# A streamed-weight ring on Trainium2: alternating its fetches between SyncE's hardware queue and GpSimd's software queue

## The chip, the cores and the metric

One core of one Trainium2 chip. The metric is the time of one execution on the device, in microseconds (us); lower is better. Each kernel was executed several times, and each execution has a state (fast or slow, by its time against the fastest of the same kernel). All times below are medians.

## The reference, cut to what matters

Two independent parts write the two halves of the output. Part A (a long convolution) is not touched by the change. Part B is a recurrence over 64 segments of 32 rows, with an 8-row memory carried from one segment to the next:

```python
for s in range(n_seg):                                # 64
    h = concat([mem, x[:, 32*s:32*s+32]], axis=1)     # 40 rows x 1024
    q, k, v = h @ Wq, h @ Wk, h @ Wv                  # 32 heads of 128
    p = softmax(where(mask, q @ k.T * scale, -1e9))
    o = (p @ v) @ Wo
    mem = o[:, :8]                                    # the next segment needs this
    outs.append(o[:, 8:])
```

Every segment needs all four weight matrices, 64 chunks of 128 x 2048 bf16 (512 KB each). They do not all fit on the chip, so some are read again for every segment.

## The kernel before

Of the 64 chunks of a segment, 44 stay in SBUF and 20 are streamed from a DRAM copy `WS` into a ring of four slots. The chunks are used in a fixed order. When TensorE has used a chunk, its slot is free, and the fetch of the chunk four places later is issued:

```python
NSTREAM = 20
RING = 4
...
ring = ctx.enter_context(tc.tile_pool(name="b_ring", bufs=RING))
...
uses = [ch for s in range(n_seg) for ch in order if ch in streamed]

def fetch():
    n = len(loaded)
    if n < len(uses):
        t = ring.tile([128, 2048], BF, tag="wring", name="wring")
        nc.sync.dma_start(t[:], stream_src(uses[n]))        # L576: SyncE, hardware queue
        loaded.append(t)

def done(ch):
    if ch in streamed:
        loaded[used[0]] = None
        used[0] += 1
        fetch()
...
class Proj:                                                 # q, k or v, one half of the heads
    def run(self, n=8):
        for kc in range(self.kc, self.kc + n):
            ch = (self.m, kc, self.g)
            w = weight(ch)
            for c in range(4):
                nc.tensor.matmul(self.acc[32*c:32*c+32, :], lhsT=hT[:, kc, :], rhs=w[:, c*512:(c+1)*512], ...)
            done(ch)
```

Each engine executes its instructions in program order, the issue of a DMA included, so it matters what else stands in GpSimd's order. In a segment, before the change:

```python
for c in range(4):                                          # at the start of the segment
    nc.gpsimd.dma_start(VBs[32*c:32*c+8, :], VBD[s, c])     # L627: values of the memory rows
... # GpSimd also copies a few keys and queries (L631, L638), twice a segment
if s + 1 < n_seg:
    load_x(s + 1)                                           # L600: rec <- REC, on GpSimd
...
nc.gpsimd.dma_start(<32 rows of out>, Y[:])                 # L793: the output of the segment
if j == NB - 1:                                             # in every fourth segment
    ...
    for dq in range(4):                                     # L798: rewrites 8 rows of each of 4 segments
        nc.gpsimd.dma_start(<out rows>, YB[32*dq:32*dq+32, :])
```

`YB` writes rows that `Y` has written, so its first store waits until the `Y` store has landed.

Of the kernel before, what the change touches and what calls it, by code (L numbers as in the profile page):

```python
# [392 lines left out]
def b_kernel(ctx: ExitStack, tc, x, mem0, Wq, Wk, Wv, Wo, outb, n_seg):  # L393
    nc = tc.nc
# [37 lines left out]
    def stream_src(ch):  # L432
        return WS[ring_order.index(ch), :, 0:2048]
# [134 lines left out]
    uses = [ch for s in range(n_seg) for ch in order if ch in streamed]  # L568
# [3 lines left out]
    def fetch():  # L572
        n = len(loaded)
        if n < len(uses):
            t = ring.tile([128, 2048], BF, tag="wring", name="wring")
            nc.sync.dma_start(t[:], stream_src(uses[n]))  # L576
            loaded.append(t)

    def weight(ch):
# [5 lines left out]
# [5 lines that stand above are left out]
# [21 lines left out]
    with tc.manual_schedule():  # L611
        for _ in range(RING):
            fetch()
# [255 lines left out]
```

## Time and profile before

| | before |
|---|---|
| time, median of the first 4 runs | 2673.66 us |
| recurrence, in the profiled run | from about 541 us to 2686 us |
| a segment | 33.3 us (mean spacing of the copies `rec<-y_tp`, one a segment; 32.8 us without the very first, which took 63.6) |
| streamed in a segment | 20 chunks of 512 KB |

First lines of the profile page of the kernel before. In the 40 slices, DMA is the mean busy share of the 16 DMA engines in tenths, and GB/s is what they moved. Then the chain of waits (the work that ended last, followed back), the groups of instructions (`busy, mean ns | idle time just before them <- what ended most of it`), and the DMA issues (`count, KB each, median us from issue to landing`).

```profile
DMA  7886945599999999999999999998999999999996
GB/s 282 307 285 247 345 142 162 176 370 334 332 337 330 348 319 332 338 330 328 329 334 333 329 329 334 329 326 312 330 332 329 328 349 322 346 324 346 334 345 248
...
q1 hardware_dynamic: 265560, 767.19, 80.8%
q0 software_dynamic: 26048, 45.25, 5.0%
...
DMA 56%; PE 31%; issue 3%; DVE 3%; ACT 1%; POOL 1%; SPq 0%; DVEq 0%; ACTq 0%; POOLq 0%
DMA wring<-WS 50%; PE acc L654 14%; PE yacc L740 6%; PE kb_ps L534 4%; PE qk_tp L669 2%; PE vb_ps L547 2%; DMA out_dram<-ot 1%; DMA Wearly<-in_B_Wk_dram 1%; ACT Y L790 1%; DMA pw<-in_B_Wv_dram 1%; PE y_tp L606 1%; DMA X_sb<-in_B_x_dram 1%; 
...
L654 PE MATMUL acc<-wring,rec 128*32 128x512 bf16 x3840 | 419.8, 425 | 371.3 <-DMA wring<-WS 366.3
...
L740 PE MATMUL yacc<-wring,OT 128*32 128x256 bf16 x2560 | 149.7, 293 | 156.4 <-DMA wring<-WS 153.3
...
wring<-WS SPq DMA_DIRECT2D x1280, 512.0 KB, 5.6
```

From slice 9 on, the DMA engines look nearly always busy, at about 330 GB/s. Half of the span lies on the DMA of `wring` in the chain of waits. TensorE, the engine of the matmuls, stood idle 366.3 and 153.3 us until a `wring` DMA had landed. Nearly all bytes are on q1, SyncE's queue; q0 is GpSimd's.

The windows view of the kernel before, over the steady part of the recurrence (columns: stretch, its length, busy us and number of instructions of PE, PEld, DVE, ACT and POOL, granted TensorE clock as a share of full speed, DMA share, GB/s):

```profile
core 0: us, PE busy (x) PEld busy (x) DVE busy (x) ACT busy (x) POOL busy (x), PEclk, DMA share, GB/s
600.00:2500.00 1900.00, 1365.37 (x28828) 682.29 (x28828) 366.19 (x1344) 391.81 (x752) 328.90 (x983) 0.91 0.94 332
```

GpSimd's instructions in order of time, kernel before, around the end of a fourth segment (start, us, instruction; in brackets the idle time before it):

```profile
1493.37 0.76 POOL L793 DMA_DIRECT2D out_dram<-Y  x1 [12.22 <-ACT Y L790]
1497.75 2.35 POOL L798 DMA_DIRECT2D out_dram<-YB  x4 [3.62 <-issue]
1500.09 2.06 POOL L627 DMA_DIRECT2D VBs<-VBD  x4
```

`Y` is issued at 1493.37. The first `YB` store waits 3.62 us; the profile names no releaser in this place. The loads of `VBs` follow only after that. The new segment began at 1493.5, so GpSimd is late by several microseconds, which costs nothing here: no weight fetch stands behind it.

### The profile page before, as it was taken

The page shows a single profiled execution, that of the slowest core. Times are in us where ns is not written, and L with a number is a line of the kernel's source. Part 1 is how long each engine was busy: PE and PEld are TensorE (multiplying, and loading weights), DVE is VectorE, ACT ScalarE, POOL GpSimd, SP SyncE. Part 2 cuts the span into 40 slices and gives each one's busy share as a digit, 9 for nine tenths or more (in the row PEclk, how much of TensorE's full clock was granted, in tenths as well). Part 3 has the DMA queues.
Part 4 walks back from the last instruction along what each step waited for, and adds up shares of the span by engine and source line. Part 5 has one row for each costly group of instructions (what it writes and reads, how often), then busy time and mean ns, then how long its engine had stood idle before and what let it go on. Part 6 is the DMA issues. An engine that isn't in the chain of part 4 may idle for free.

```text
span 2686.0 us, 76248 instructions
## 1 busy us (share of the span) xinstructions
PE 1844.0 (69%) x33598; PEld 904.9 (34%) x33620; DVE 659.9 (25%) x1944; ACT 639.8 (24%) x1143; POOL 461.6 (17%) x1210
## 2 busy tenths in 40 slices
PE   3565298837777767767776777676776767677765
PEld 1221143313333333333333333333433333333333
DVE  5896221101111111111121112111111111111111
ACT  6873011112222222222222222221222222222221
POOL 5043000001211111111111111111111111212111
PEclk9797599968899998989899889888889898998998
DMA  7886945599999999999999999998999999999996
GB/s 282 307 285 247 345 142 162 176 370 334 332 337 330 348 319 332 338 330 328 329 334 333 329 329 334 329 326 312 330 332 329 328 349 322 346 324 346 334 345 248
DMA packets 302324, 841.52 MB, mean 313 GB/s; under 512 B 72396, under 2 KB 84716, under 8 KB 301991
## 3 DMA queue, kind: packets, MB, share of 16 engines
q1 hardware_dynamic: 265560, 767.19, 80.8%
q0 software_dynamic: 26048, 45.25, 5.0%
q10 hardware_dynamic: 10384, 24.20, 2.6%
q8 instruction: 262, 4.29, 0.6%
q14 instruction: 70, 0.57, 0.1%
HBM read 777.14 MB, written 61.87 MB: 312 GB/s over the span
## 4 chain that ended last, share of the span: by engine, by line
DMA 56%; PE 31%; issue 3%; DVE 3%; ACT 1%; POOL 1%; SPq 0%; DVEq 0%; ACTq 0%; POOLq 0%
DMA wring<-WS 50%; PE acc L654 14%; PE yacc L740 6%; PE kb_ps L534 4%; PE qk_tp L669 2%; PE vb_ps L547 2%; DMA out_dram<-ot 1%; DMA Wearly<-in_B_Wk_dram 1%; ACT Y L790 1%; DMA pw<-in_B_Wv_dram 1%; PE y_tp L606 1%; DMA X_sb<-in_B_x_dram 1%; POOL Yre L342 1%; DVE rec L607 0%; DMA Wlate<-in_B_Wv_dram 0%
## 5 line engine op out<-in xcount | busy, mean ns | idle before, releaser
L654 PE MATMUL acc<-wring,rec 128*32 128x512 bf16 x3840 | 419.8, 425 | 371.3 <-DMA wring<-WS 366.3
L654 PEld LDWEIGHTS <-rec 128*32 128x32 bf16 x12288 | 339.9, 103 | 850.0 <-issue 646.3
L663 ACT CAST qkv_sb<-acc 128x512 bf16<-128x512 f32 x384 | 224.7, 585 | 1066.3 <-PE acc L654 1066.3
L654 PE MATMUL acc<-Wearly,rec 128*32 128x512 bf16 x4608 | 436.0, 461 | 32.3 <-DVE rec L607 21.3
L654 PE MATMUL acc<-Wlate,rec 128*32 128x512 bf16 x3840 | 333.3, 390 | 0.0
L740 PEld LDWEIGHTS <-OT 128*32 128x32 bf16 x8192 | 235.5, 100 | 236.2 <-issue 220.1
L740 PE MATMUL yacc<-Wlate,OT 128*32 128x256 bf16 x5632 | 274.0, 286 | 13.0 <-issue 13.0
L740 PE MATMUL yacc<-wring,OT 128*32 128x256 bf16 x2560 | 149.7, 293 | 156.4 <-DMA wring<-WS 153.3
L631 POOL COPY KT<-rec 128x128 bf16<-128x128 bf16 x128 | 38.2, 298 | 710.8 <-PE S L680 635.6
L754 DVE COPY KT<-qk_tp 128x512 bf16<-128x512 bf16 x64 | 27.2, 425 | 514.2 <-PE qk_tp L669 514.2
L793 POOL DMA_DIRECT2D out_dram<-Y x64 | 48.4, 756 | 565.4 <-ACT Y L790 520.9
L627 POOL DMA_DIRECT2D VBs<-VBD x256 | 128.9, 510 | 0.7 <-issue 0.4
L600 POOL DMA_DIRECT2D rec<-REC x64 | 37.2, 581 | 451.4 <-PE acc L654 324.7
L790 ACT CAST Y<-yacc 128x256 bf16<-128x256 f32 x64 | 23.8, 372 | 375.5 <-PE yacc L740 375.5
L607 DVE COPY rec<-y_tp 128x64 bf16<-128x64 bf16 x64 | 12.3, 192 | 410.8 <-PE y_tp L606 402.9
L685 DVE TENSOR_REDUCE mx<-S 128x5 f32<-128x200 f32 x128 | 47.1, 368 | 258.2 <-PE S L680 257.9
L669 PE MATMUL qk_tp<-ident,qkv_sb 128*128 128x128 bf16 x1024 | 108.5, 233 | 0.5 <-ACT KT L763 0.5
L722 ACT CAST OT<-OTp 128x512 bf16<-128x512 f32 x128 | 74.9, 585 | 138.0 <-PE OTp L713 135.8
L740 PE MATMUL yacc<-Wlate,OTB 128*32 128x256 bf16 x1408 | 91.8, 283 | 15.5 <-issue 13.9
L669 PEld LDWEIGHTS <-qkv_sb 128*128 128x128 bf16 x1024 | 62.7, 102 | 109.8 <-issue 82.0
L726 DVE CAST OTB<-OTp 128x128 bf16<-128x128 f32 x128 | 34.7, 271 | 221.9 <-ACT OT L722 221.9
L534 PE MATMUL kb_ps<-XBT,Wearly 128*128 128x512 bf16 x283 | 83.9, 385 | 1.7 <-ACT XBT L501 1.2
(192 smaller groups left out, 2134.6 us busy)
## 6 DMA issues: line engine op xcount, KB each, us to landing
wring<-WS SPq DMA_DIRECT2D x1280, 512.0 KB, 5.6
rec<-REC POOLq DMA_DIRECT2D x64, 192.0 KB, 5.7
SK<-s_sb SPq DMA_DIRECT2D x16, 512.0 KB, 4.1
SU<-s_sb SPq DMA_DIRECT2D x16, 512.0 KB, 3.7
Kg<-SK ACTq DMA_DIRECT2D x32, 256.0 KB, 4.0
Ug<-SU SPq DMA_DIRECT2D x32, 256.0 KB, 5.0
REC<-stage SPq DMA_DIRECT2D x4, 2048.0 KB, 13.2
pw<-in_B_Wv_dram SPq DMA_DIRECT2D x16, 512.0 KB, 6.3
```

What stands on the lines that cost most here:

```text
L534: nc.tensor.matmul(ps[:], lhsT=ws[kc][:, hl * 128:(hl + 1) * 128], rhs=XBT[:, kc].rearrange("p s t -> p (s t)"), start=(kc == 0), stop=(kc ...
L547: nc.tensor.matmul(ps[:], lhsT=XBT[:, kc, 16 * tb:16 * tb + 16, :].rearrange("p s t -> p (s t)"), rhs=ws[kc][:, c * 512:(c + 1) * 512], st ...
L627: nc.gpsimd.dma_start(VBs[32 * c:32 * c + 8, :], VBD[s, c])
L631: nc.gpsimd.tensor_copy(KT[:, :, :, 32:40], KBs[:, 128 * g:128 * g + 128].rearrange("p (c i t) -> p i c t", c=4, i=4))
L654: nc.tensor.matmul(self.acc[32 * c:32 * c + 32, :], lhsT=hT[:, kc, :], rhs=w[:, c * 512:(c + 1) * 512], start=(kc == 0), stop=(kc == 7), t ...
L663: nc.scalar.copy(sb[:], self.acc[:])
L669: nc.tensor.transpose(tp[:, i * 128:(i + 1) * 128], sb[:, i * 128:(i + 1) * 128], ident[:])
L685: nc.vector.tensor_reduce(out=mx[:], in_=S, op=ALU.max, axis=AX.X)
L722: nc.scalar.copy(OT[:], o_view(g)[:, :, :, 0:32])
L740: nc.tensor.matmul(yacc[32 * dq:32 * dq + 32, o:o + 256], lhsT=src, rhs=w[:, hh * 1024 + dq * 256:hh * 1024 + (dq + 1) * 256], start=(h == ...
L790: nc.scalar.copy(Y[:], yacc[:, 0:256])
L793: nc.gpsimd.dma_start(bass.AP(outb.tensor, outb.offset + SEG * s * 2048, [[256, 4], [2048, 32], [1, 256]]), Y[:])
```

## The change

The intent: issue the fetches from two engines, so that two DMA queues work on the stream.

```diff
         n = len(loaded)
         if n < len(uses):
             t = ring.tile([128, 2048], BF, tag="wring", name="wring")
-            nc.sync.dma_start(t[:], stream_src(uses[n]))
+            (nc.sync if n % 2 == 0 else nc.gpsimd).dma_start(t[:], stream_src(uses[n]))
             loaded.append(t)
```

Even chunks stay on SyncE, odd ones go to GpSimd. Bytes, slots and the order of use are the same.

## The prediction

> **What bounds the kernel now.** The recurrence (about 541 to 2675 us of the profiled 2686.0) is paced by streamed weights. The chain of waits puts 50% of the span on the DMA of `wring`. The windows view shows the 16 DMA engines 94% busy there, at 332 GB/s. The memory-row copies (`rec<-y_tp`) come every 33.3 us, one a segment: 20 chunks of 512 KB, 1.65 us each. It is a closed loop of four slots: SyncE issues chunk n+4 about 0.02 us after TensorE's last matmul on chunk n; issue to landing is 5.6 us median (DMA issues view). TensorE waits on `wring` 366+153 us (groups view).
>
> **What changes.** Ten of a segment's 20 chunks move from SyncE's in-order stream to GpSimd's. No byte, buffer or wait is removed. The Trainium skill, "DMA: Bandwidth & Descriptors", section "Issuing engines are not separate DMA queues", says all queues run on the same 16 engines, so I expect no new bandwidth; what is saved is SyncE's 0.32 us of issue a chunk, and SyncE is not the limit. 512 KB issues on GpSimd take 0.53 us in the trace and land about as fast as SyncE's (6.8 and 6.3 us for `pw`; 7.0 and 7.5 for `zt`). GpSimd is 17% busy, so 640 x 0.53 = 340 us more fits; no VectorE lock-out shows: `VBs` issues take 497 to 544 ns throughout.
>
> **What hurts: order on GpSimd.** A fetch now stands behind whatever GpSimd waits for.
> - Three of four segments: after the output `Y`, four `VBs` issues end 2.5 us into the segment; the first odd fetch was issued at 2.8 to 3.0 us. Hardly any delay.
> - After every fourth segment (15 that matter): the four `YB` stores wait until `Y` has landed (about 5 us), then take 2.35 us, then `VBs` 2.1 us. GpSimd is free about 10 us into the next segment, today harmless. Its first odd fetch (index 5), today issued at 2.0 us and used at 8.6 us, is then issued at 10 to 12 us and used at 15 to 17. SyncE can fetch only chunks 4, 6 and 8 meanwhile, since TensorE consumes in order; the DMA engines run dry for 5 to 7 us. Because DMA is the limit, most is not made up: 7 us x 15, about +105 us.
> - The two streams interleave, so an even chunk finishes later than in one first-in-first-out queue; with four slots the loop has little slack. Estimate 0 to +3% of 2130 us; I take +30 us. Two rings may instead hide gaps (the bulk load on two hardware queues at 537 to 566 us reached 387 GB/s), which would offset this.
>
> All of this is on the critical path, because chunk waits are.
>
> **Prediction.** 2673.6 + 105 + 30 = about 2810 us, range 2720 to 2920. Faster by over 2%: 0.05; within 2%: 0.11; slower by over 2%: 0.84.
>
> **What would show it.** Segments following a `YB` store grow from 33.5 to about 40 us, the others by under 1 us; in them the first GpSimd `wring` issue comes 10 to 12 us in, the DMA share dips, and TensorE has one `wring` wait of over 5 us. About 335 MB move from q1 to q0.
>
> **What would make it wrong.** Two rings lifting the rate above 345 GB/s in the other segments (then within 2% or faster); a GpSimd stall that I don't see, such as issues much above 0.53 us or fetches held by earlier software DMAs, adding over 1 us to every segment (then above 2900); or the ring refilling quickly after the gap, so that only 3 us a time is lost.

## The result, and the profile after

| | before | after |
|---|---|---|
| time, median of 4 runs | 2673.66 us | 2862.61 us |
| ratio | | 1.0709 (95% interval 1.0654 to 1.0764) |
| GB/s, 600 to 2500 us | 332 | 306 |
| first memory copy (start of the recurrence) | 541.8 us | 550.9 us |
| segment after a `YB` store (mean of 15) | 31.46 us | 38.30 us |
| the other segments of four, in order | 32.17, 33.09, 34.63 us | 34.21, 33.95, 35.51 us |

A ratio is the mean time of one kernel's fast runs over that of the other's of the same rounds, so it is not quite the ratio of the quoted medians. The segment lengths were worked out from the trace as the spacing of the 64 copies `rec<-y_tp`; the mean of the segments after a `YB` store leaves out the very first segment of the run, which took over 60 us in both kernels.

The same lines of the page of the changed kernel:

```profile
DMA  8887946789888889898888888989898889898886
GB/s 281 306 274 257 319 113 186 271 309 324 308 308 292 300 269 320 287 322 310 310 303 306 287 307 304 317 302 326 291 320 305 303 301 325 309 324 304 316 311 244
...
q1 hardware_dynamic: 173400, 431.61, 42.0%
q0 software_dynamic: 118208, 380.84, 39.4%
...
DMA 59%; PE 24%; issue 6%; POOL 5%; DVE 2%; ACT 2%; SPq 0%; POOLq 0%; DVEq 0%; ACTq 0%
DMA wring<-WS 51%; PE acc L654 10%; PE yacc L740 5%; PE kb_ps L534 4%; DMA out_dram<-Y 3%; POOL VBs L627 2%; PE vb_ps L547 2%; POOL out_dram L798 1%; ACT s_sb L232 1%; DMA out_dram<-ot 1%; PE qk_tp L669 1%; DMA Wearly<-in_B_Wk_dram 1%; DMA 
...
L654 PE MATMUL acc<-wring,rec 128*32 128x512 bf16 x3840 | 437.4, 442 | 483.9 <-DMA wring<-WS 479.5
L576 POOL DMA_DIRECT2D wring<-WS x640 | 341.0, 533 | 1482.6 <-PE acc L654 745.7
...
L740 PE MATMUL yacc<-wring,OT 128*32 128x256 bf16 x2560 | 156.0, 305 | 189.8 <-DMA wring<-WS 186.2
...
wring<-WS POOLq DMA_DIRECT2D x640, 512.0 KB, 5.4
wring<-WS SPq DMA_DIRECT2D x640, 512.0 KB, 5.5
```

380.84 - 45.25 = 335.6 MB have moved from q1 to q0, as they should. The rate fell in nearly every slice of the recurrence, not only in some. TensorE now waits 479.5 and 186.2 us on `wring`. The 640 fetches on GpSimd cost 533 ns of its time each and land as fast after their issue (5.4 us) as SyncE's (5.5 us).

```profile
600.00:2500.00 1900.00, 1288.99 (x26693) 648.65 (x26690) 337.51 (x1243) 361.57 (x694) 581.50 (x1435) 0.86 0.88 306
```

This row is from the windows view of the changed kernel, with the columns given above; the DMA engines are now busy 0.88 of the time, and TensorE's granted clock is lower too (0.86 against 0.91), while it is idle more.

GpSimd's instructions of the changed kernel around the end of a fourth segment (the new one begins at 1434.6), and below them, from TensorE's part of the timeline, the matmuls that waited for the late chunk:

```profile
1441.31 2.37 POOL L798 DMA_DIRECT2D out_dram<-YB  x4 [5.94 <-DMA out_dram<-Y]
1443.67 2.06 POOL L627 DMA_DIRECT2D VBs<-VBD  x4
1445.72 1.11 POOL L576 DMA_DIRECT2D wring<-WS  x2
```

```profile
1441.89 0.40 PE L654 MATMUL acc<-wring,rec 128*32 128x512 bf16 x4 [1.76 <-DMA wring<-WS]
...
1449.70 0.62 PE L654 MATMUL acc<-wring,rec 128*32 128x512 bf16 x4 [5.78 <-DMA wring<-WS]
```

The two `wring` fetches now stand behind `YB`'s wait of 5.94 us, the four `YB` stores and the four `VBs` loads. They start at 1445.72, 11 us into the segment, and TensorE waits 5.78 us. Six microseconds of this gap, from 6 to 12 us into the segment, and the corresponding six of the kernel before, each from the windows view:

```profile
1440.60:1446.60 6.00, 2.03 (x20) 0.77 (x20) 0.42 (x1) 0.58 (x1) 5.29 (x10) 0.67 0.52 177
```

```profile
1499.50:1505.50 6.00, 5.18 (x60) 2.06 (x57) 0.85 (x2) 1.17 (x2) 3.52 (x11) 0.74 0.98 329
```

The DMA engines ran at half their share in the gap. So the delay that the prediction described is there. Whether it is the cause of the loss is another question, and the segments that have no such gap are longer too.

What GpSimd waited for, changed kernel (waits view: `engine line <- releaser: us in total, times, longest us`):

```profile
POOL wring L576 <- PE acc L654: 745.7, 324, 42.0
POOL wring L576 <- PE yacc L740: 479.0, 187, 6.5
POOL wring L576 <- DMA wring<-WS: 219.8, 68, 5.4
...
POOL out_dram L798 <- DMA out_dram<-Y: 83.5, 16, 6.9
```

The wait of `YB` sums to 83.5 us over 16 times.

### The profile page after: what moved, and what is told of

It reads as the page before. It is cut to its first block, busy times and chain, and to the rows that moved or that the text cites. A ratio compares the mean times of both kernels' runs of the same rounds, so it can differ in the third digit from the quotient of the medians.

```text
span 2858.7 us, 76125 instructions
## 1 busy us (share of the span) xinstructions
PE 1881.4 (66%) x33620; PEld 921.0 (32%) x33620; DVE 659.6 (23%) x1944; ACT 639.6 (22%) x1143; POOL 796.4 (28%) x1850
## 3 DMA queue, kind: packets, MB, share of 16 engines
q0 software_dynamic: 118208, 380.84, 39.4%
## 4 chain that ended last, share of the span: by engine, by line
DMA 59%; PE 24%; issue 6%; POOL 5%; DVE 2%; ACT 2%; SPq 0%; POOLq 0%; DVEq 0%; ACTq 0%
DMA wring<-WS 51%; PE acc L654 10%; PE yacc L740 5%; PE kb_ps L534 4%; DMA out_dram<-Y 3%; POOL VBs L627 2%; PE vb_ps L547 2%; POOL out_dram L798 1%; ACT s_sb L232 1%; DMA out_dram<-ot 1%; PE qk_tp L669 1%; DMA Wearly<-in_B_Wk_dram 1%; DMA pw<-in_B_Wv_dram 1%; DMA SK<-s_sb 1%; DMA X_sb<-in_B_x_dram 1%
## 5 line engine op out<-in xcount | busy, mean ns | idle before, releaser
L654 PE MATMUL acc<-wring,rec 128*32 128x512 bf16 x3840 | 437.4, 442 | 483.9 <-DMA wring<-WS 479.5
L576 POOL DMA_DIRECT2D wring<-WS x640 | 341.0, 533 | 1482.6 <-PE acc L654 745.7
L654 PE MATMUL acc<-Wlate,rec 128*32 128x512 bf16 x3840 | 353.1, 413 | 0.0
L740 PEld LDWEIGHTS <-OT 128*32 128x32 bf16 x8192 | 245.7, 104 | 268.2 <-issue 242.2
L740 PE MATMUL yacc<-Wlate,OT 128*32 128x256 bf16 x5632 | 285.6, 297 | 7.5 <-issue 7.5
L740 PE MATMUL yacc<-wring,OT 128*32 128x256 bf16 x2560 | 156.0, 305 | 189.8 <-DMA wring<-WS 186.2
L757 DVE COPY QT<-qk_tp 128x512 bf16<-128x512 bf16 x64 | 27.2, 424 | 368.1 <-PE qk_tp L669 368.1
L638 POOL COPY QBm<-rec 128x32 bf16<-128x32 bf16 x512 | 83.2, 208 | 0.0
```

The source lines that it names most:

```text
L576: (nc.sync if n % 2 == 0 else nc.gpsimd).dma_start(t[:], stream_src(uses[n]))
L638: nc.gpsimd.tensor_copy(q[:, :, 40 * i:40 * i + 8], QBs[:, 128 * g:128 * g + 128].rearrange("p (c i t) -> p c i t", c=4, i=4)[:, :, i, :])
L654: nc.tensor.matmul(self.acc[32 * c:32 * c + 32, :], lhsT=hT[:, kc, :], rhs=w[:, c * 512:(c + 1) * 512], start=(kc == 0), stop=(kc == 7), t ...
L740: nc.tensor.matmul(yacc[32 * dq:32 * dq + 32, o:o + 256], lhsT=src, rhs=w[:, hh * 1024 + dq * 256:hh * 1024 + (dq + 1) * 256], start=(h == ...
```

## The experiments

Three theories were tested. Theory A is the prediction's: the fetches are held up by what stands before them in GpSimd's order. Theory L: a fetch on GpSimd starts later after its slot comes free than one on SyncE, and four slots leave no room for that. Theory I: two queues that share the DMA engines serve a chunk and its successor at once, so that chunks land unevenly; this costs whatever the second queue is. In the first call L and I together were the rival B. The runs came in three calls, and each call has its own runs of the kernel before: yb_late, vbs_spread, both_moved and control_sp (2681.98 us); gpsimd_all, act_alt, sp_delay2 and ring5 (2682.63 us); act_delay1, halves_act, ring5_alt and ring6 (2676.40 us). So runs are best compared by their ratios.

| run | median us | ratio to before, 95% interval | GB/s, 600 to 2500 us |
|---|---|---|---|
| changed kernel | 2862.61 | 1.0709, 1.0654 to 1.0764 | 306 |
| yb_late | 2844.22 | 1.0596, 1.0545 to 1.0648 | 311 |
| vbs_spread | 2884.11 | 1.0751, 1.0713 to 1.0789 | 305 |
| both_moved | 2842.66 | 1.0607, 1.0542 to 1.0671 | 311 |
| control_sp | 2691.12 | 1.0031, 1.0001 to 1.0061 | 332 |
| gpsimd_all | 2770.18 | 1.0319, 1.0285 to 1.0353 | 321 |
| act_alt | 2797.25 | 1.0401, 1.0354 to 1.0448 | 315 |
| sp_delay2 | 2731.33 | 1.0182, 1.0132 to 1.0232 | 325 |
| act_delay1 | 2826.64 (one of four runs slow) | 1.0537, 1.0484 to 1.0590 | 316 |
| halves_act | 3497.15 | 1.3019, 1.2920 to 1.3118 | 238 (slow profile) |
| ring5 | 2536.62 | 0.9444, 0.9412 to 0.9477 | 377 |
| ring5_alt | 2821.92 | 1.0522, 1.0466 to 1.0578 | 328 |
| ring6 | 2572.21 | 0.9606, 0.9571 to 0.9640 | 387 |

All gave correct results. Apart from the profile of halves_act, the profiles compared are of fast runs.

### Taking the waits out of GpSimd's order

**yb_late**: the `YB` stores go half a segment later, when `Y` has long landed.

```diff
             if s + 1 < n_seg:
                 load_x(s + 1)
+            store_yb()                      # the YB stores kept back from the segment before, if any
             V1 = pv1.evac()
 ...
-                for dq in range(4):
-                    nc.gpsimd.dma_start(<out rows>, YB[32 * dq:32 * dq + 32, :])
+                late_yb.append((b, YB))
+                if s + 1 == n_seg:
+                    store_yb()
```

> The changed kernel with one edit: the four YB stores are issued half a segment later in GpSimd's order, when the Y store has long landed, so that GpSimd no longer waits there. Theory A (order on GpSimd): the segments after a YB store fall from 38.3 us to about 32.5 us, 15 of them, so about 2770 us (2755 to 2790), ratio to the kernel before 1.03 to 1.045. Theory B (the software queue, or two interleaved queues, is itself slower, in every segment): no change worth the name, 2840 to 2875 us, ratio about 1.07.

Measured: 2844.22 us, ratio 1.0596. In the waits view of yb_late, `YB` waits for `Y` once, 3.0 us, at the very end, instead of 16 times and 83.5 us. The median fell by 18 us from that of the changed kernel (about 30 us by the ratios), not by 90. The segments after a `YB` store did fall, from 38.30 to 35.70 us, but the other three of each four rose a little, to 34.59, 34.94 and 35.74 us. The four issues of the `YB` stores still stand in GpSimd's order, only later and without the wait. Theory A's main term is a small part of the loss.

**vbs_spread**: the `VBs` loads, one after each of the first four projections.

```diff
-            for c in range(4):
+            def load_vbs(c):
                 nc.gpsimd.dma_start(VBs[32 * c:32 * c + 8, :], VBD[s, c])
 ...
             k0 = Proj(0, 0).run().evac()
+            load_vbs(0)
             q0 = Proj(1, 0).run().evac()
+            load_vbs(1)
 ...                                         # (2) after k1, (3) after q1
```

> The changed kernel with one edit: the four VBs loads no longer stand together before the first fetch of a segment but one each after the four projections, so no fetch stands behind more than one. Theory A: the first odd fetch goes out 0.7 us earlier in the 48 ordinary segments (each about 1 us shorter, about -45 us) and 2 us earlier after a YB store (15 x 2 = -30 us): about 2790 us, 2770 to 2820. Theory B: no change, 2840 to 2875 us.

Measured: 2884.11 us, ratio 1.0751. No gain; the intervals of this and of the changed kernel overlap. A miss for theory A. But the edit is not free: TensorE now waits 29.2 us for `VBs` (34 waits, waits view of vbs_spread), where the changed kernel has no such wait, so a small gain may be hidden.

**both_moved**: both edits.

> The changed kernel with both edits (YB stores late, VBs loads spread). Theory A: nearly all of the loss gone, 2690 to 2730 us; what is left is the slower start (+9 us) and what interleaving costs. Theory B: at least 2800 us. If it comes out below 2670 us, two queues are a gain once GpSimd's order is out of the way.

Measured: 2842.66 us, ratio 1.0607. With both obstacles taken out of the way, 6.1 of the 7.1% stay, spread over all segments (35.16, 34.41, 34.94 and 36.03 us, in the order of the table above). The spread `VBs` loads cost something here too, a wait that none of the kernel before, the changed kernel, yb_late and control_sp has (waits view of both_moved):

```profile
PE OTp L724 <- DMA VBs<-VBD: 23.3, 30, 1.8
```

That is a small part of the 160 us by which the median is above the kernel before. Theory A falls as the explanation of the whole. The windows view of both_moved:

```profile
600.00:2500.00 1900.00, 1309.13 (x27073) 658.57 (x27072) 346.48 (x1272) 369.06 (x708) 598.49 (x1459) 0.87 0.89 311
```

**control_sp**: the same two edits in the kernel before.

> Control: the kernel before (all fetches on SyncE) with the same two edits of GpSimd's order. Both theories: same as the kernel before within 1%, 2650 to 2690 us, since no fetch stands on GpSimd. If it is clearly faster, the two edits help by themselves and the gain of both_moved must be read against this run.

Measured: 2691.12 us, ratio 1.0031. Within 1%, as expected by both theories; the edits gain nothing by themselves.

### One queue, two queues, and a late start, each by itself

**gpsimd_all**: one queue, the software one; the small loads and stores go to SyncE.

```diff
-            (nc.sync if n % 2 == 0 else nc.gpsimd).dma_start(t[:], stream_src(uses[n]))
+            nc.gpsimd.dma_start(t[:], stream_src(uses[n]))
 ...                                         # rec, VBs, Y and YB: nc.gpsimd -> nc.sync
```

> All 1280 fetches on GpSimd's software queue and the small loads and stores of the recurrence (rec, VBs, Y, YB) on SyncE: one queue again, first in first out, but the software one. Theory L (start latency: a fetch on GpSimd reaches its first packet about 0.8 us later after TensorE's release than one on SyncE, and with four slots in a closed loop of 6.6 us that is lost rate): every loop is the slow one, so about 7.0 us a loop and 2830 to 2900 us. Theory I (interleaving two queues is what costs, because a chunk and its successor share the engines and land together): one queue again, so 2670 to 2730 us.

Measured: 2770.18 us, ratio 1.0319. Between the two expectations: all fetches on the software queue cost less than half of what alternating with it costs (3.2 against 7.1%). So the software path is a part, and not the whole.

**act_alt**: two queues, both hardware.

```diff
-            (nc.sync if n % 2 == 0 else nc.gpsimd).dma_start(t[:], stream_src(uses[n]))
+            (nc.sync if n % 2 == 0 else nc.scalar).dma_start(t[:], stream_src(uses[n]))
```

> The alternation kept, but the odd fetches go through ScalarE's hardware queue, GpSimd's order as in the kernel before. Theory L: the hardware start is fast, so 2670 to 2720 us. Theory I: two queues interleave as in the changed kernel, so 2800 to 2860 us. If two hardware queues hide gaps, below 2650 us.

Measured: 2797.25 us, ratio 1.0401. Just below the range of theory I, and slower than SyncE's or GpSimd's queue alone, with no software path at all. So alternation itself costs. A part of the 4.0% has another cause: ScalarE's copy `Y` now follows a fetch in ScalarE's order, and TensorE's waits for it sum to 55.0 us instead of 29.8. The waits view of act_alt:

```profile
PE acc L654 <- DMA wring<-WS: 378.3, 327, 4.7
PE yacc L740 <- DMA wring<-WS: 179.0, 165, 3.4
PE y_tp L606 <- ACT Y L790: 55.0, 63, 1.0
```

and of the kernel before:

```profile
PE y_tp L606 <- ACT Y L790: 29.8, 63, 0.5
```

**sp_delay2**: the kernel before with a later start of the odd fetches, by means of two loads of 32 bytes ahead of each.

```diff
-            t = ring.tile([128, 2048], BF, tag="wring", name="wring")
+            tt = ring.tile([128, 2048 + 64], BF, tag="wring", name="wring")
+            t = tt[:, 0:2048]
+            if n % 2 == 1:
+                for z in range(2):
+                    nc.sync.dma_start(tt[0:1, 2048+16*z:2048+16*z+16], stream_src(uses[n])[0:1, 0:16])
-            nc.sync.dma_start(t[:], stream_src(uses[n]))
+            nc.sync.dma_start(t, stream_src(uses[n]))
```

> The kernel before, all on SyncE, with two one-row loads of 32 bytes into spare columns of the slot ahead of every odd fetch, after the same wait for the slot: two more issues of 0.32 us, so an odd fetch starts about 0.64 us later and nothing else changes. Theory L: most of the loss appears with no software queue and no interleaving, about 2780 to 2830 us. Theory I, or the view that the DMA engines are simply full: 2670 to 2710 us.

Measured: 2731.33 us, ratio 1.0182. A start that is 0.58 us later for every second chunk (1.01 us instead of 0.43 from TensorE's last matmul on the slot, medians of the odd fetches) costs 49 us of 2682. The interval lies above 1, so the cost is real, though by the 2% rule the verdict is unclear. It lies between the two expected ranges: smaller than theory L alone wanted.

**act_delay1**: act_alt with one such load ahead of each odd fetch, on ScalarE's queue.

```diff
+            q = nc.sync if n % 2 == 0 else nc.scalar
+            if n % 2 == 1:
+                q.dma_start(tt[0:1, 2048:2064], stream_src(uses[n])[0:1, 0:16])
-            nc.sync.dma_start(t[:], stream_src(uses[n]))
+            q.dma_start(t, stream_src(uses[n]))
```

> The alternation of SyncE and ScalarE, with one 32-byte load ahead of each odd fetch (about 0.3 us later start, which is what a GpSimd fetch shows against one on SyncE: 0.70 against 0.43 us after the last matmul on the slot). If the loss of the changed kernel is alternation plus a later start plus little else, this rebuilds it without the software queue: 2815 to 2850 us, near both_moved (2843). If the software queue has a cost of its own beyond its start, this stays at 2790 to 2810 us.

Measured: 2826.64 us, ratio 1.0537. The number is in the expected range, and its interval overlaps with that of both_moved (1.0484 to 1.0590 and 1.0542 to 1.0671). The agreement does not show what it was meant to show, though. In act_delay1 a fetch and its extra load stand ahead of the copy `Y` on ScalarE (waits view):

```profile
PE y_tp L611 <- ACT Y L795: 73.2, 63, 1.4
```

In both_moved this wait is 29.9 us. TensorE's waits for `wring`, on the other hand, are no longer than in act_alt, and shorter than in both_moved (the table at the end of the next section). So two sums of different parts came out alike. What the software queue costs beyond its later start is not shown.

### The loop of a slot, from the trace

For each fetch the trace gives the start of TensorE's last matmul on the chunk that held the slot before, the issue, the landing (last semaphore update), and the first matmul on the new chunk. Means over the segments that do not follow a `YB` store, in us; worked out from the traces, not lines of a view:

| run, queue | last matmul to issue | issue to landing | landing to use | sum |
|---|---|---|---|---|
| before, SyncE | 0.44 | 5.67 | 0.43 | 6.54 |
| gpsimd_all, GpSimd | 0.75 | 5.67 | 0.32 | 6.74 |
| sp_delay2, SyncE, even and odd | 0.75 | 5.52 | 0.40 | 6.66 |
| act_alt, SyncE / ScalarE | 0.47 / 0.45 | 5.66 / 5.74 | 0.72 / 0.63 | 6.85 / 6.83 |
| both_moved, SyncE / GpSimd | 0.46 / 0.74 | 5.66 / 5.71 | 0.87 / 0.50 | 6.99 / 6.95 |
| changed kernel, SyncE / GpSimd | 0.46 / 0.76 | 5.65 / 5.66 | 0.77 / 0.44 | 6.88 / 6.86 |

In a segment every slot is used five times, and there are 64 segments, so 0.1 us on the loop is 0.1 x 5 x 64 = 32 us on the kernel. The sum follows the length of the segment by construction, whatever makes the segment long (a fifth of it, less the matmuls on the chunk itself), so it explains nothing by itself. The stages tell where in the loop the time went. The time from issue to landing hardly moves. Two other stages do:

- A fetch on GpSimd is issued 0.3 us later after the slot is free (0.75 against 0.44). With all fetches on GpSimd the loop grows by 0.20 us; with half of them, an estimate from these numbers is 0.1 to 0.15 us.
- With two queues a landed chunk waits longer for its turn (0.43 to about 0.68 in act_alt). One reason shows in the steps between the landings of successive chunks. On one queue (before, gpsimd_all) no step is under 0.8 us and 11% are over 2.4 us. In act_alt 12% are under 0.8 and 20% over 2.4; in both_moved 19% and 24%, and there an even chunk follows its predecessor after 1.10 us on average and an odd one after 2.36. So chunks land in pairs: the second of a pair sits in its slot and waits for the first to be used, and a slot that waits is not being filled.

In both_moved the later issue is 0.16 us on average of the two queues, the longer wait for the turn 0.26, and the sum grows by 0.43 (6.97 against 6.54), which is 138 us of the 154 by which its profiled run is longer. About 10 us more are the later start of the recurrence (first memory copy at 552.3 instead of 541.8 us).

That chunks are served at once can be read from the packets. Each chunk is 128 packets of 4096 bytes, so the packets of a queue can be assigned to chunks by their order (worked out from the trace of act_alt, same segments; the 5% of packets that start first and last are left out). In act_alt 62% of the chunks overlap their predecessor, which is on the other queue, by more than 0.3 us, and both queues have packets in service 75% of the time. So both queues are served at once, as theory I says.

How much of the loss that makes up is less clear, since a landed chunk also waits longer when TensorE is held up elsewhere. TensorE's own account, in us per segment, means over the 62 segments between the second memory copy and the last (worked out from the traces):

| run | segment | TensorE busy | waits for `wring` | waits for `Y` | waits for `VBs` | granted clock |
|---|---|---|---|---|---|---|
| before | 32.83 | 23.56 | 7.69 | 0.47 | 0 | 0.908 |
| gpsimd_all | 34.00 | 23.78 | 8.85 | 0.47 | 0 | 0.906 |
| act_alt | 34.45 | 24.01 | 8.70 | 0.87 | 0 | 0.876 |
| act_delay1 | 34.63 | 24.05 | 8.51 | 1.16 | 0 | 0.875 |
| both_moved | 35.12 | 24.18 | 9.33 | 0.47 | 0.35 | 0.873 |
| changed kernel | 35.45 | 24.11 | 10.03 | 0.47 | 0 | 0.863 |

Of the 1.62 us by which a segment of act_alt is longer, 1.01 are waits for `wring`, 0.40 the late `Y`, and 0.45 longer matmuls at a lower granted clock (other waits shrank by about 0.2). The clock is lower in all four kernels that alternate, and not in gpsimd_all, where TensorE waits for `wring` about as long as in act_alt. Why it is lower, and whether the time would come back at the old clock or turn into waiting, was not tested.

### Is it the queues as such?

**halves_act**: each chunk in two halves, one on each hardware queue, so that two queues are busy but chunks keep their order.

```diff
-            nc.sync.dma_start(t[:], stream_src(uses[n]))
+            nc.sync.dma_start(t[0:64, :], stream_src(uses[n])[0:64])
+            nc.scalar.dma_start(t[64:128, :], stream_src(uses[n])[64:128])
```

> All from hardware queues: every chunk is fetched as two halves of 64 rows, one on SyncE's and one on ScalarE's queue, so that two queues are busy at once but chunks are still served in their order. If alternation costs because successive chunks share the engines and land in pairs or out of order (theory I): the cost is gone, 2660 to 2720 us. If two busy queues as such are slower on the DMA engines: as the alternation of SyncE and ScalarE, 2770 to 2820 us.

Measured: 3497.15 us, ratio 1.3019. Neither expectation: the experiment failed to keep the rest constant. The 4096-byte packets, of 159 ns median in the kernel before (trace), took 279 ns here, with the DMA engines at full share and 238 GB/s. (The profiled execution was slow, at 3530 us; the fast ones took 3464 to 3513.) In act_alt, where by the trace each of the two queues was active 87% of the time and both at once 75%, the median stayed at 159 ns (and the mean at 185, 183 before). So two busy queues alone do not make packets that slow; the 64-row shape of the transfers, and twice as many of them, differ too. The run therefore says nothing about the order of service. That two queues serving chunks in order would cost nothing is not shown.

### Is the DMA full?

The prediction took the DMA engines' share of 0.94 to mean that bandwidth was the limit.

**ring5**: the kernel before with a fifth slot, paid for with a resident chunk.

```diff
-NSTREAM = 20
+NSTREAM = 21
-RING = 4
+RING = 5
```

> The kernel before with five slots instead of four, paid for with one resident chunk less, so 21 instead of 20 chunks are streamed in a segment (5% more bytes). If the recurrence was limited by what four slots keep in flight (theory L): rate up from 332 to 370 GB/s or more, 2520 to 2640 us. If the DMA engines were full at 332 GB/s, as the prediction took them to be: 5% more bytes cost 5% of 2130 us, about 2780 us.

Measured: 2536.62 us, ratio 0.9444. Five per cent more bytes in 5.6% less time. The windows view of ring5:

```profile
600.00:2500.00 1900.00, 1423.86 (x31214) 717.47 (x31207) 395.18 (x1453) 423.49 (x813) 356.52 (x1063) 0.96 1.00 377
```

377 GB/s against 332: the DMA engines had not been at their limit. By the trace 3.44 of 4 slots were in flight on average before, and 4.37 of 5 in ring5 (issue to landing, 600 to 2500 us). The recurrence was limited by what four slots keep in flight; a busy share of 0.94 did not show that. The packets had been slower at four slots: 183 ns on average against a median of 159, with 1% over 760 ns; with five slots 170 on average and 1% over 421. So some of the busy time was probably waiting; the trace does not tell for what.

**ring5_alt**: the changed kernel with the same two numbers changed.

> The changed kernel with five slots and 21 streamed chunks a segment. If the loss is latency in a closed loop that keeps too little in flight, a fifth slot hides part of it: ratio to ring5 (2537 us) below 1.07, about 2600 to 2680 us, and faster than the kernel before. If the loss is a lower rate of the DMA engines with two queues, it stays at 7% of ring5 or more, 2710 us or above.

Measured: 2821.92 us, ratio 1.0522, which is 11% above ring5 (1.0522 / 0.9444). The expectation that a fifth slot hides part of the loss is refuted: alternating costs more here, not less. The unevenness is greater: 23% of the steps between landings are under 0.8 us (none in ring5), and segments after a `YB` store take 38.07 us against 29.80. Only 3.85 of five slots are in flight. What the `YB` wait and what alternation contribute here was not separated.

**ring6**: six slots, 22 streamed chunks.

> The kernel before with six slots and 22 streamed chunks. Four slots moved 332 GB/s and five 361 (5.6% less time); with six the rate should come near the 387 to 400 GB/s of the bulk load, 22 chunks of 512 KB at 385 GB/s are 30.0 us a segment, about the same as the 29.3 to 29.8 of ring5: 2500 to 2570 us. It shows where more in flight stops paying.

Measured: 2572.21 us, ratio 0.9606; 387 GB/s. Somewhat slower than ring5: the rate rises by 3% and the bytes by 5%. Both beat the two kernels; ring5, with all fetches on SyncE, is the fastest version measured.

## Why the prediction was right or wrong

The measured 2862.61 us lies in the stated range of 2720 to 2920, and the direction was right. The sum holds partly by compensation: one term was far too large, the other far too small, and that the total came out in the range is in part luck.

- *"What hurts: order on GpSimd", +105 us from the fourth segments.* The picture was right in detail: the first odd fetches that stand behind `YB` went out 10.7 and 11.2 us after the end of the memory copy of such segments, were used first at 14.7 us (8.4 before), and the segments grew by 6.84 us (15 x 6.84 = 103 us). But this is not what the wait costs. With the wait taken away (yb_late) the kernel gained 18 us by medians, 1.1 points of ratio. This is the term that was mis-sized: 105 us predicted, 18 us (medians) to 30 us (ratios) measured. Most of the length of those segments belongs to the cost that every segment has (both_moved: 35.16 us in them, where before has 31.46), and some came back as longer other segments. Why the other segments lengthen when the gap is removed was not settled.
- *"Hardly any delay" in three of four segments.* At the first fetch it was small: 3.2 to 3.7 us into the segment instead of 2.7 to 2.9. Spreading the `VBs` loads brought no gain, with a wait of 29.2 us of its own, so at most this order mattered little. But the forecast that these segments grow by under 1 us failed for the first of the three (2.04 us; 0.86 and 0.88 for the others).
- *"Estimate 0 to +3% ...; I take +30 us" for interleaving and a late start.* This is the main term and was far too small: both_moved, where little else is left (23.3 us of waits for `VBs` and 10 us of a later start), is 6.1% above before. The runs split it into an alternation that costs with hardware queues alone (act_alt, 4.0%, part of it ScalarE's own order), and a later start of GpSimd's fetches (gpsimd_all 3.2% with all of them; sp_delay2 1.8% for 0.58 us on half of them). That these parts add up to both_moved's loss, with nothing left for the software queue itself, was not shown.
- *"DMA is the limit".* Wrong as read. Four slots in flight were the limit (ring5). In such a loop every tenth of a microsecond between free slot and use of the new chunk counts, which is why a 0.3 us later issue and unevenly landing chunks can cost so much. The sentence "with four slots the loop has little slack" had the right idea and the wrong size. The Trainium skill, "Perfetto Trace Analysis", section "Identifying the Most-Contended Engine", says not to judge DMA by occupancy, since with 16 DMA engines it misleads. The prediction did just that; ring5 agrees with the page: a share of 0.94 went with 332 GB/s, and 377 could be had.
- *"I expect no new bandwidth".* Right. The Trainium skill, "DMA: Bandwidth & Descriptors", section "Issuing engines are not separate DMA queues", says that all queues share the same DMA engines. The trace agrees as far as it goes: bytes moved from q1 to q0, and the rate did not rise but fell, from 332 to 306 GB/s. The fear that two rings might hide gaps was not borne out at four slots or at five.
- *"No VectorE lock-out shows".* Right. The Trainium skill, "SBUF — State Buffer", warns in its box on the "DVE blocks DMA" trap that GpSimd cannot write descriptors while a VectorE instruction of certain modes holds the port pair that the two share. Here the 640 issues on GpSimd took 527 to 576 ns, none longer.
- The same DMA page, section "Latency and other measured facts", gives a later first byte for the software path (about 1 us against about 0.6). The trace agrees in direction: the earliest first packet came 1.23 us after the issue in gpsimd_all and 0.95 us in the kernel before, and the issue itself comes 0.3 us later after the slot is free. From issue to landing no difference is left (5.67 us in both): in the full ring a fetch mostly queues, and on average its first packet comes 2.6 us (gpsimd_all) and 2.5 us (before) after the issue.

## What to carry to other kernels

In this kernel, a ring whose chunks are used in order did best on one queue that serves them in order; a second queue added no bandwidth and made chunks land in pairs, which holds slots that should be filling. Before calling a stream limited by bandwidth, count the slots in flight and try one more: here a DMA share of 0.94 was a latency limit, and a fifth slot was worth 5.6% although it meant 5% more bytes. And a gap that is plain to see in the trace still has to be taken away to learn its price: this one measured 6.8 us in each of 15 segments, and its removal gave back less than a third of it. An experiment whose total agrees must still be read wait by wait: act_delay1 matched both_moved with other waits.

## What the Trainium skill lacked or had wrong

- "DMA: Bandwidth & Descriptors", rules for kernel authors: spreading DMAs over issuing engines is said not to help bandwidth. It doesn't say that it can cost: alternating an in-order stream between two hardware queues took 4.0% more time (act_alt, a part of it a late copy on ScalarE), between SyncE and GpSimd 6.1 to 7.1%.
- The same rules say of two transfers to disjoint partition halves not to bother, and don't say that they can cost. With two 64-row halves on two hardware queues instead of one 128-row transfer the kernel took 30% longer; in its profile, of a run in the slow state, the 4096-byte packets took 279 ns instead of 159. Why is open.
- The page tells rate by transfer size, and not by number of transfers in flight. Here, with 512 KB each on one hardware queue, four slots moved 332 GB/s, five 377 and six 387.
- "Perfetto Trace Analysis", section "What 'DMA-bound' means", lists DMA engines, the issuing sequencer and SBUF reads as what may bind. A closed loop of a few buffers is not on that list (though the page's section "Optimization Strategy" names the buffer count as a possible reason for gaps that repeat): 3.44 of four slots in flight at 332 GB/s and a busy share of 0.94; 4.37 of five at 377 and 1.00.
